# Block sums of x on GpSimd or VectorE, copies of x out of one PSUM tile in sequence, and a new compute order for the front

## The chip, the cores and the metric

The kernel runs on one core of a Trainium2 chip. The core has a matrix engine (TensorE, PE in the profile; PEld is its weight load), three engines for element-wise work (VectorE = DVE, ScalarE = ACT, GpSimd = POOL), and SyncE (SP), which here only issues DMAs. Each engine runs its own instructions strictly in program order and waits on semaphores for the others. Operands lie in SBUF (128 partitions); matmul results lie in PSUM, in eight banks. The metric is the device time of one execution in microseconds, the median of several.

## What is computed

Linear attention with the feature map elu+1 on 8 batches of 8 heads, 576 tokens, 64 features; its output, laid out as 4608 tokens of 512 features, goes through a mixture of 8 experts whose routing weights are balanced by eight Sinkhorn rounds.

```python
def _attn_ref(q, k, v):                       # (8, 8, 576, 64)
    def phi(x): return np.where(x > 0, x, np.exp(x) - 1.0) + 1.0
    q_p, k_p = (phi(q), phi(k))
    kv = np.einsum('bhsd,bhse->bhde', k_p, v)
    z = np.sum(k_p, axis=2)
    num = np.einsum('bhsd,bhde->bhse', q_p, kv)
    den = np.einsum('bhsd,bhd->bhs', q_p, z)[..., None] + 1e-06
    return (num / den)
def _moe_ref(x, w_gate, w1, w2):              # 4608 tokens, D 512, E 8, F 1024
    P = np.exp(logits - logits.max())         # logits = x @ w_gate; then 8 rounds of row and column scaling
    for e in range(E):
        h = np.maximum(x @ w1[e], 0.0)
        out += P[:, e:e + 1] * (h @ w2[e])
```

## The kernel before, in words

**Stages.** The *front* (0 to about 121 us of the span) is the attention, in 16 half batches (`att(b, g)`, n = 2b + g, each one batch and four heads). The matrix work of the first expert on the first token groups is mixed in between as filler. Then come the other experts. Tokens are worked in 9 groups g of 512. For expert 0 the groups 0 to 4 are done plainly: `layer1` (L637, hq: x times w1, then relu L641 on ACT) and the second layer (L906, ye: h times w2, then a copy to `acc`, L260 on ACT or L262 on DVE). Groups 5 to 8 of expert 0 and all later experts use a seven-product (Strassen-like) scheme for the first layer, `block7` (L783, L788), and, for later experts, for the second (L1044). From 170 us on the matrix work of all later experts runs in one fixed sequence.

**One half batch of the front.** DMAs bring k and q (one tile `kqin`, two buffers) and v (`vin`, two buffers). From n = 2 to 5 all three, and later v alone, are issued from POOL's queue; the others from SP's. ACT takes exp of k and of q (L311), DVE forms max(1 + x, 1) (L324, fp32 in, fp16 out) and then min with the exp (L327, two fp16 tiles of SBUF in). v is copied to `vv` (L260 on ACT or L262 on DVE). PE forms k'v (L356), copied to `kvz` by either engine; PE turns q over (L212), copied to `qpT` by either engine. PE forms the numerators and denominators (L414, in two parts); 1e-6 is added (`rden`, L424 on ACT or L426 on DVE), DVE takes the reciprocal (L429) and multiplies (`xn`, L438). PE turns `xn` over into one PSUM tile (L212), and two copies take it to `xT` in SBUF: `f_xc`, one instruction for s = 0 and one for s = 1, on ACT (L260) or DVE (L262). For n = 0 the two lie in two tiles, for n > 0 in one.

**Block sums.** The seven-product scheme needs sums and differences of blocks of x. `x_blocks(g)` makes four tiles T[0] to T[3] from `xT` of its 512 tokens with four subtractions of 128 x 512 fp16 (L675, L676 in the first task, i = 0; L678 in the second; L680 in the third), all on DVE. `f_st` and `f_raw` then send T and x to DRAM from SP's queue (tile `xd`); later experts read them back from there (`x_load`, L712). Groups 0 to 4 ("early") put T into a part of the accumulator tile `acc[6]`, two halves in turn; groups 5 to 8 into `xst`, two buffers, after the memory of the front is free (`t_close`), and expert 0 reads these T directly in `block7`. The column `acc` in the profile's L675 to L680 rows is this use of `acc[6]`.

**The order.** Every piece of work is a task with a number, dependencies, buffer groups, and a planned cost for each engine that may run it (`_Plan.add`). `_Plan.run(order)` takes a text with one list of task numbers for each engine: pool, pe, sp, dma (planned transfers, no instruction), act and dve. A task with several engines in its cost table runs on the one whose list holds it. Within an engine the list is the program order. The dependencies in the plan only shape the sequence in which the tasks are written out; the semaphores are placed by the tile framework from the real reads and writes, and two engines that read one PSUM tile are also put in sequence. The lists cover the front, expert 0 and the start of expert 1; the rest follows from priorities in the plan, with the matrix work of the later experts chained in one fixed sequence.

Of the kernel before, what the change touches and what calls it, by code (L numbers as in the profile page):

```python
# [139 lines left out]
def kernel(  # L140
# [136 lines left out]
    def att(b, g):  # L277
# [186 lines left out]
        for s in range(2):  # L464
            w, o = (256, 320)[s], S * b + 256 * s

            def f_xc(e, s=s, w=w, o=o):
                copy(e, xT[:, 2 * g:2 * g + 2, o:o + w],
                     gxn["ps"][s][:, 0:640].rearrange("p (c t) -> p c t", c=2)[:, :, 0:w])
            t2 = fadd({"act": (0.56, 0.65)[s], "dve": (0.38, 0.46)[s]}, f_xc, deps=[t1], use=[gxs[s % len(gxs)]], prio=pr)  # L470
            for c2 in range(2):
                xt_done.setdefault((b, 2 * g + c2), []).append(t2)

# [178 lines left out]
    def x_blocks(g):  # L652
# [9 lines left out]
                nc.sync.dma_start(out=xd[g // 2][:, g % 2, 1 + b], in_=xT[:, 2:4, t0 + 256 * b:t0 + 256 * b + 256])  # L662
        last = first = None
        for i in range(3):
            def f_T(_, i=i):
                if i == 0 and early:
                    h_ = (len(p_xse["order"]) - 1) % 2
                    gt_["tile"] = (acc[NA - 1][:, 2 * h_:2 * h_ + 2, :].bitcast(FP16)
                                   .rearrange("p a (b c t) -> p (a b) c t", b=2, c=2))
                elif i == 0:  # L670
                    gt_["tile"] = accp[2].tile([P, 4, 2, 256], FP16, tag="xst", name="xst")
                T = gt_["tile"]
                lo, hi = xT[:, :, t0:t0 + 256], xT[:, :, t0 + 256:t0 + 512]
                if i == 0:
                    nc.vector.tensor_tensor(out=T[:, 0], in0=hi[:, 0:2], in1=lo[:, 0:2], op=ALU.subtract)  # L675
                    nc.vector.tensor_tensor(out=T[:, 2], in0=hi[:, 2:4], in1=hi[:, 0:2], op=ALU.subtract)  # L676
                elif i == 1:
                    nc.vector.tensor_tensor(out=T[:, 1], in0=hi[:, 2:4], in1=T[:, 0], op=ALU.subtract)  # L678
                else:
                    nc.vector.tensor_tensor(out=T[:, 3], in0=lo[:, 2:4], in1=T[:, 1], op=ALU.subtract)  # L680
            last = add(("dve", 0.8 if i == 0 else 0.42), f_T,
                       deps=deps + [v_land[NG + 1 + g] if early else t_close, last] +
                       ([xst_of[g - 1][2]] if i == 0 and g > NG - NL else []),
                       acq=[gt_] if i == 0 else [], use=[gt_], prio=g - 8.0)
            first = first or last
            x_users.append(last)
# [455 lines left out]
    for d, k_ in zip(chain, chain[1:]):  # L1142
        S_.dep(k_, d)

    order = """
        pool 0 50 102 104 106 108 110 137 139 141 169 171 175 177 554 179 206 208 210 241 272 305 336 367 398 431 462
        493 524 534 586 583 1571 1091 1580 1573 1582 1584 1575 1119 1117 1093 1577 1240 1216 1586 1214 1242 1337 1339
        1363 1365
        pe 2 3 4 5 6 7 8 9 10 11 12 13 14 15 16 17 18 51 54 19 20 21 22 62 23 58 24 25 26 86 83 94 27 28 29 30 31 90 66
# [24 lines left out]
        act 42 43 75 76 82 87 84 68 112 113 100 143 629 631 144 637 121 150 639 633 152 635 641 643 127 654 181 136 182  # L1174
# [11 lines left out]
        dve 44 46 45 49 47 55 77 56 52 78 63 59 64 79 80 65 60 61 88 91 95 67 92 96 93 114 97 115 116 99 119 117 124 145  # L1186
# [15 lines left out]
    """  # L1202
    S_.run(order)

# [29 lines left out]
```

## Time and profile before

| | |
|---|---|
| time, median of 3 runs | 953.49 us (953.34 to 954.19) |
| the profiled execution | 953.06 us; its span from first to last instruction 951.2 us |
| busy in the span | PE 938.1 us (99%), DVE 768.6 us (81%), ACT 565.1 us (59%), POOL 161.7 us (17%) |
| granted TensorE clock | 1.000 |
| the 36 block-sum subtractions on DVE (L675 to L680) | 0.40 to 0.42 us each |
| two-input adds on POOL (L1068, 128 x 256 fp32), x124 | 852 ns mean, 726 ns median |

The profiled execution lies 0.43 us under the median of the runs; the span is 1.86 us shorter than the execution's own time. A matmul's end is modelled, 380 ns after its start for 512 columns, although the next one starts 216 ns after it; so short pauses of PE are hidden in its busy time, and the distance from one start to the next is the better reading.

### The profile page before, as it was taken

Reading aid. Unit: us, or ns where it says so; the run is one execution under the profiler, and the core shown is the slowest. Engines: PE = TensorE matmul, PEld = TensorE weight load, DVE = VectorE, ACT = ScalarE, POOL = GpSimd, SP = SyncE. Lnnn points to the kernel's source line nnn. Section 1 sums busy time; section 2 is a strip of 40 time slices with the busy share of each in tenths; the row PEclk is TensorE's granted clock in tenths of the full one; section 3 lists DMA queues with packets and bytes.
Section 4 is the critical chain, followed back from the end, with each engine's and each line's share of the span. In section 5 each row is a group of like instructions: output and inputs, shape, how many; then the busy total and the mean of one; then the engine's idle time right before and its main releaser. Section 6 shows DMA issues by size and latency. Waiting matters only on the chain.

```text
span 951.2 us, 19287 instructions
## 1 busy us (share of the span) xinstructions
PE 938.1 (99%) x7524; PEld 631.7 (66%) x7524; DVE 768.6 (81%) x1527; ACT 565.1 (59%) x1023; POOL 161.7 (17%) x209
## 2 busy tenths in 40 slices
PE   6999999999999999999999999999999999999998
PEld 3555567466676667766676667766676666766676
DVE  6899988788887787878887787887877788877776
ACT  4799755665655555555555555555555555555551
POOL 3211100022222211221112211221112211111111
PEclk9999999999999999999999999999999999999999
DMA  9998965253254422544145431644125532425545
GB/s 310 302 270 245 222 193 182 50 103 85 65 149 111 111 68 62 111 111 101 57 132 116 102 84 44 135 111 101 56 77 103 109 96 56 139 79 161 150 107 133
DMA packets 109948, 118.91 MB, mean 125 GB/s; under 512 B 7840, under 2 KB 95520, under 8 KB 109856
## 3 DMA queue, kind: packets, MB, share of 16 engines
q1 hardware_dynamic: 81600, 90.33, 31.2%
q0 software_dynamic: 27856, 26.82, 16.9%
q8 instruction: 59, 0.97, 0.4%
q10 hardware_dynamic: 400, 0.52, 0.2%
q14 instruction: 33, 0.27, 0.1%
HBM read 119.69 MB, written 17.69 MB: 144 GB/s over the span
## 4 chain that ended last, share of the span: by engine, by line
PE 94%; DMA 2%; ACT 1%; DVE 1%; issue 0%; SPq 0%; DVEq 0%; ACTq 0%
PE ye L1044 34%; PE hq L783 20%; PE att L783 10%; PE ye L906 6%; PE Zye L1044 6%; PE Zye L783 5%; PE hq L788 4%; PE hq L637 3%; PE att L788 2%; DMA kqin<-in_k_dram 1%; PE Zye L788 1%; DMA vin<-in_v_dram 1%; PE kv_ps L212 1%; PE kv_ps L356 1%; PE kv_ps L414 1%; DVE xn L438 0%
## 5 line engine op out<-in xcount | busy, mean ns | idle before, releaser
L1058 DVE SCALAR_TENSOR_TENSOR acc<-ye,P_sb,acc 128x256 f32<-128x256 f32 x620 | 267.3, 477 | 101.9 <-PE ye L1044 99.9
L1044 PEld LDWEIGHTS <-S 128*128 128x128 f16 x1984 | 194.1, 98 | 45.9 <-issue 0.3
L1068 POOL TENSOR_TENSOR acc<-acc,h 128x256 f32<-128x256 f32 x124 | 103.6, 852 | 601.2 <-ACT h L1065 595.8
L1044 PE MATMUL ye<-h,S 128*128 128x256 f16 x1488 | 192.8, 273 | 0.0
L1044 PEld LDWEIGHTS <-h 128*128 128x128 f16 x1488 | 145.6, 98 | 39.9
L823 ACT ACTIVATE h<-hq 128x512 f16<-128x512 f32 x134 | 80.1, 598 | 137.1 <-PE hq L783 116.9
L783 PEld LDWEIGHTS <-W 128*128 128x128 f16 x896 | 87.7, 98 | 81.2
L783 PE MATMUL att<-xs,W 128*128 128x512 f16 x448 | 133.2, 379 | 0.0
L783 PE MATMUL hq<-xs,W 128*128 128x512 f16 x448 | 133.2, 379 | 0.0
L783 PE MATMUL hq<-xs,w 128*128 128x512 f16 x448 | 124.1, 379 | 0.0
L826 DVE CUSTOM_DVE_ANT_0 h<-att,s 128x512 f16<-128x512 f32 x126 | 86.2, 686 | 21.8 <-ACT s L810 19.2
L783 PEld LDWEIGHTS <-w 128*128 128x128 f16 x672 | 65.8, 98 | 54.5
L820 ACT ACTIVATE h<-Zye 128x512 f16<-128x512 f32 x134 | 80.1, 597 | 34.0 <-PE Zye L783 28.1
L803 ACT COPY Zye<-hq 128x512 f32<-128x512 f32 x134 | 77.9, 581 | 33.5 <-PE hq L783 26.8
L826 DVE CUSTOM_DVE_ANT_0 h<-hq,s 128x512 f16<-128x512 f32 x126 | 86.4, 686 | 12.3 <-PE hq L783 12.2
L1065 ACT ACTIVATE h<-Zye,P_sb 128x256 f32<-128x256 f32 x124 | 52.3, 470 | 72.5 <-PE Zye L1044 72.5
L810 ACT COPY s<-hq 128x512 f32<-128x512 f32 x126 | 73.5, 584 | 35.0 <-PE hq L783 30.6
L1015 DVE TENSOR_TENSOR S<-h 128x1024 f16<-128x1024 f16 x124 | 85.1, 687 | 6.9 <-ACT h L823 6.9
L817 ACT COPY s<-att 128x512 f32<-128x512 f32 x126 | 74.6, 592 | 1.3 <-PE att L783 1.3
L906 PE MATMUL ye<-w,h 128*128 128x512 f16 x296 | 74.2, 380 | 0.0
L783 PE MATMUL Zye<-xs,w 128*128 128x512 f16 x224 | 66.6, 379 | 0.0
L1044 PE MATMUL ye<-w,h 128*128 128x256 f16 x496 | 64.3, 273 | 0.0
(123 smaller groups left out, 1048.8 us busy)
## 6 DMA issues: line engine op xcount, KB each, us to landing
xs<-xd SPq DMA_DIRECT2D x196, 256.0 KB, 4.2
w<-in_moe_w_dram POOLq DMA_DIRECT2D x48, 256.0 KB, 4.3
out_dram<-acc SPq DMA_DIRECT2D x67, 128.0 KB, 2.4
kqin<-in_k_dram SPq DMA_DIRECT2D x12, 576.0 KB, 5.6
kqin<-in_q_dram SPq DMA_DIRECT2D x12, 576.0 KB, 7.1
xs<-xd SPq DMA_DIRECT2D x49, 128.0 KB, 2.7
xd<-xT SPq DMA_DIRECT2D x27, 128.0 KB, 3.2
vin<-in_v_dram POOLq DMA_DIRECT2D x10, 288.0 KB, 6.8
```

What stands on the lines that cost most here:

```text
L783: nc.tensor.matmul(dst, lhsT=lhs(0, c), rhs=X(b)(c), start=(first and c == 0), stop=(c == 1), skip_group_check=True)
L803: nc.scalar.copy(out=Zt[1], in_=gX["tile"])
L810: nc.scalar.copy(out=gs2["tile"], in_=gX["tile"])
L817: nc.scalar.copy(out=gs5["tile"], in_=gR["tile"])
L820: nc.scalar.activation(out=hd(0, 0), in_=Zt[1], func=AF.Relu)
L823: nc.scalar.activation(out=hd(1, 0), in_=gX["tile"], func=AF.Relu)
L826: nc.vector._custom_dve(TENSOR_ADD_SAT, out=dst, in0=ps, in1=sb, s0=3.0e38, s1=0.0)
L906: nc.tensor.matmul(gy[tt]["tile"], lhsT=hx(f, P * tt, P), rhs=gw2["tile"][:, f, :], start=(f == 0), stop=(f == NFT - 1))
L1015: nc.vector.tensor_tensor(out=gS[i]["tile"], in0=a0, in1=a1, op=op)
L1044: nc.tensor.matmul(bank(g_)[:, s, :], lhsT=lhs(s, kk), rhs=rhs(kk), start=(new and s == 0 and kk == 0), stop=(kk == 3), skip_group_check=True)
L1058: nc.vector.scalar_tensor_tensor(out=dst(), in0=bank(g_)[:, s, :], scalar=P_sb[:, gg, e:e + 1], in1=dst(), op0=ALU.mult, op1=ALU.add)
L1068: nc.gpsimd.tensor_tensor(out=dst(), in0=dst(), in1=gst["tile"], op=ALU.add)
```

## The change

Three parts.

1. `x_blocks`: the four subtractions of a group may run on POOL as well as on DVE. In the new lists POOL runs 28 of the 36: all four of the groups 0, 1, 2, 4, 6 and 8, and the first two of the groups 3 and 7. The rest (the last two of groups 3 and 7, all of group 5) stay on DVE. 18 of the 28 belong to early groups.
2. `f_xc`: in the plan, the copy of s = 1 depends on the copy of s = 0 when both come from one PSUM tile.
3. The lists for pool, pe, act and dve are replaced. The lists for sp and dma are as they were. 35 tasks go from ACT to DVE and 35 from DVE to ACT (copies, `rden` additions, one `xn`, scalings of `acc`); the rest changes place only.

```diff
-            t2 = fadd({"act": (0.56, 0.65)[s], "dve": (0.38, 0.46)[s]}, f_xc, deps=[t1], use=[gxs[s % len(gxs)]], prio=pr)
+            t2 = fadd({"act": (0.56, 0.65)[s], "dve": (0.38, 0.46)[s]}, f_xc, deps=[t1, t2 if s and n else None], use=[gxs[s % len(gxs)]], prio=pr)
...
-            def f_T(_, i=i):
+            def f_T(eng, i=i):
...
+                v_ = nc.gpsimd if eng == "pool" else nc.vector
                 lo, hi = xT[:, :, t0:t0 + 256], xT[:, :, t0 + 256:t0 + 512]
                 if i == 0:
-                    nc.vector.tensor_tensor(out=T[:, 0], in0=hi[:, 0:2], in1=lo[:, 0:2], op=ALU.subtract)
-                    nc.vector.tensor_tensor(out=T[:, 2], in0=hi[:, 2:4], in1=hi[:, 0:2], op=ALU.subtract)
+                    v_.tensor_tensor(out=T[:, 0], in0=hi[:, 0:2], in1=lo[:, 0:2], op=ALU.subtract)
+                    v_.tensor_tensor(out=T[:, 2], in0=hi[:, 2:4], in1=hi[:, 0:2], op=ALU.subtract)
...
-            last = add(("dve", 0.8 if i == 0 else 0.42), f_T,
+            last = add({"dve": 0.75 if i == 0 else 0.42, "pool": 3.6 if i == 0 else 1.8}, f_T,
...
-        pool 0 50 102 104 106 108 110 137 139 141 169 171 175 177 554 179 206 208 210 241 272 305 336 367 398 431 462
-        493 524 534 586 583 1571 1091 1580 1573 1582 1584 1575 1119 1117 1093 1577 1240 1216 1586 1214 1242 1337 1339
+        pool 0 50 102 104 106 108 110 137 139 141 169 171 175 177 554 179 206 208 210 241 272 305 336 367 398 588 589
+        431 590 462 595 596 493 597 524 602 534 586 603 604 609 616 583 617 848 849 850 900 618 952 953 954 1571 1091
```

In the pool list 367 and 398 are the v loads of n = 10 and 11; 431, 462, 493 and 524 those of n = 12 to 15; 534 waits for v of n = 15; 586 and 583 load weights of expert 1, 1571 of expert 2. 588 to 590 are the three tasks of group 0, 595 to 597 of group 1, 602 to 604 of group 2, 609 the first of group 3, 616 to 618 of group 4, 848 to 850 of group 6, 900 the first of group 7, 952 to 954 of group 8.

More of the change, by code (lines that the diff above doesn't have):

```diff
@@ L672, in f_T @@
                 T = gt_["tile"]
+                v_ = nc.gpsimd if eng == "pool" else nc.vector
                 lo, hi = xT[:, :, t0:t0 + 256], xT[:, :, t0 + 256:t0 + 512]
                 if i == 0:
-                    nc.vector.tensor_tensor(out=T[:, 0], in0=hi[:, 0:2], in1=lo[:, 0:2], op=ALU.subtract)
-                    nc.vector.tensor_tensor(out=T[:, 2], in0=hi[:, 2:4], in1=hi[:, 0:2], op=ALU.subtract)
+                    v_.tensor_tensor(out=T[:, 0], in0=hi[:, 0:2], in1=lo[:, 0:2], op=ALU.subtract)
+                    v_.tensor_tensor(out=T[:, 2], in0=hi[:, 2:4], in1=hi[:, 0:2], op=ALU.subtract)
                 elif i == 1:
-                    nc.vector.tensor_tensor(out=T[:, 1], in0=hi[:, 2:4], in1=T[:, 0], op=ALU.subtract)
+                    v_.tensor_tensor(out=T[:, 1], in0=hi[:, 2:4], in1=T[:, 0], op=ALU.subtract)
                 else:
-                    nc.vector.tensor_tensor(out=T[:, 3], in0=lo[:, 2:4], in1=T[:, 1], op=ALU.subtract)
-            last = add(("dve", 0.8 if i == 0 else 0.42), f_T,
+                    v_.tensor_tensor(out=T[:, 3], in0=lo[:, 2:4], in1=T[:, 1], op=ALU.subtract)
+            last = add({"dve": 0.75 if i == 0 else 0.42, "pool": 3.6 if i == 0 else 1.8}, f_T,
                        deps=deps + [v_land[NG + 1 + g] if early else t_close, last] +
@@ L1145 @@
     order = """
-        pool 0 50 102 104 106 108 110 137 139 141 169 171 175 177 554 179 206 208 210 241 272 305 336 367 398 431 462
-        493 524 534 586 583 1571 1091 1580 1573 1582 1584 1575 1119 1117 1093 1577 1240 1216 1586 1214 1242 1337 1339
-        1363 1365
-        pe 2 3 4 5 6 7 8 9 10 11 12 13 14 15 16 17 18 51 54 19 20 21 22 62 23 58 24 25 26 86 83 94 27 28 29 30 31 90 66
[11 rows of a table removed]
+        pool 0 50 102 104 106 108 110 137 139 141 169 171 175 177 554 179 206 208 210 241 272 305 336 367 398 588 589
+        431 590 462 595 596 493 597 524 602 534 586 603 604 609 616 583 617 848 849 850 900 618 952 953 954 1571 1091
+        1580 1573 1582 1584 1575 1119 1117 1093 1577 1240 1216 1586 1214 1242 1337 1339 1363 1365
+        pe 2 3 4 5 6 7 8 9 10 11 12 13 14 15 16 17 18 54 51 62 19 58 20 86 21 22 23 24 83 25 66 94 90 26 27 624 28 29
[11 rows of a table added]
         1159 1161 1163 1100 1167 1169 1165 1171 1175 1177 1103 1173 1181 1183 1179 1110 1112 1115 1185 1120 1123 1187
@@ L1173 @@
         1587 1387 1389 1391 1502 1504 1506 1508
-        act 42 43 75 76 82 87 84 68 112 113 100 143 629 631 144 637 121 150 639 633 152 635 641 643 127 654 181 136 182
[11 rows of a table removed]
-        dve 44 46 45 49 47 55 77 56 52 78 63 59 64 79 80 65 60 61 88 91 95 67 92 96 93 114 97 115 116 99 119 117 124 145
[15 rows of a table removed]
+        act 42 43 75 52 76 88 91 95 67 97 112 113 100 629 631 143 637 144 121 150 639 152 635 633 641 127 643 654 181
[11 rows of a table added]
+        dve 44 46 47 49 45 77 56 55 79 78 59 63 80 60 64 61 65 82 87 84 92 68 96 93 114 99 116 119 117 145 115 146 147
[14 rows of a table added]
     """
```

73 rows, old and new, of the table order are left out of this document.

## The prediction

> **What bounds the kernel now.** I read the busy time by stage first, since the page's averages mix them.
>
> ```profile
> core 0: us, PE busy (x) PEld busy (x) DVE busy (x) ACT busy (x) POOL busy (x), PEclk, DMA share, GB/s
> 0.00:27.00 27.00, 19.56 (x235) 9.51 (x236) 17.61 (x39) 13.60 (x15) 11.95 (x21) 1.00 1.00 311
> 27.00:67.00 40.00, 39.79 (x573) 20.49 (x572) 36.86 (x73) 35.01 (x56) 5.88 (x8) 1.00 1.02 289
> 67.00:121.00 54.00, 53.10 (x857) 28.54 (x856) 49.54 (x109) 45.96 (x72) 5.67 (x8) 1.00 0.96 233
> 121.00:170.00 49.00, 48.63 (x349) 33.44 (x347) 43.12 (x104) 27.00 (x51) 0.74 (x1) 1.00 0.55 173
> 170.00:951.00 781.00, 777.05 (x5518) 539.77 (x5516) 621.42 (x1206) 443.50 (x832) 137.47 (x171) 1.00 0.41 100
> ```
>
> From 170 us on PE has no room (in the chain of waits its matmuls follow each other at 109 ns per 256 columns). Before 27 us the inputs are on their way (DMA share 1.00). The front from 27 to 121 us is where the change can act: DVE is busy 86.4 of 94 us there, ACT 81.0, POOL 11.6. PE looks full, but its ends are modelled, so I count its work from matmul groups.
>
> ```profile
> L637 PE MATMUL hq<-xT,w 128*128 128x512 f16 x80 | 20.2, 380 | 0.0
> L906 PE MATMUL ye<-w,h 128*128 128x512 f16 x77 | 19.4, 381 | 0.0
> ```
>
> These are the groups of 67 to 121. Four such matmuls follow each other in 0.87 us, so 157 need 34.1 us. The small ones, by the least distance from one task's start to the next in the timeline: 8 k'v at 0.53, 16 turnings at 0.27, 8 pairs of numerators at 0.32, 3 logits at 0.90, together 13.8. That is 47.9 of 54 us, so PE has about 6 us of pauses here; the same count for 27 to 67 gives 36.3 of 40. Both lists of PE hold the same work up to the last logits of the front, and behind it PE is full: a microsecond by which the front gets shorter or longer is a microsecond of the kernel, and the pauses cap the gain at 10 us. DVE's largest groups in 67 to 121 (two-input min and max of the front), then its longest waits in 27 to 121 (us in total, times, longest):
>
> ```profile
> L327 DVE TENSOR_TENSOR t<-t,e 128x1152 f16<-128x1152 f16 x14 | 10.4, 750 | 0.2
> L324 DVE TENSOR_SCALAR t<-kqin 128x1152 f16<-128x1152 f32 x12 | 9.2, 769 | 0.1
> ```
>
> ```profile
> DVE xT L262 <- ACT xT L260: 2.5, 6, 0.6
> DVE rden L426 <- PE kv_ps L414: 2.1, 4, 1.1
> ```
>
> DVE waits only 5.9 us in all; it is the fullest engine, and 2.5 us of its waiting is for ACT's copy out of the same PSUM tile.
>
> **Part by part. Off DVE.** Block sums stand on DVE like this:
>
> ```profile
> 87.96 0.42 DVE L675 TENSOR_TENSOR acc<-xT 128x512 f16<-128x512 f16 x1
> 88.30 0.42 DVE L676 TENSOR_TENSOR acc<-xT 128x512 f16<-128x512 f16 x1
> 88.64 0.41 DVE L675 TENSOR_TENSOR acc<-xT 128x512 f16<-128x512 f16 x1
> ```
>
> Each lasts 0.42 us but the next starts 0.34 after it; I take 0.08 off every DVE duration for this. DVE's list up to its last x copy held 17 subtractions and holds none now: -17 x 0.336 = -5.7 us.
>
> **Between ACT and DVE.** Counted in the two lists up to the same point, with the rows' means: DVE gets 4 `qpT` copies (0.753), 3 `vv` copies (1.65 together), 2 copies to `acc` (0.678); it loses 2 `kvz` (0.421), 4 `rden` (0.164) and one `xn` (0.688): +3.8, less 0.1 for overlap. DVE's net is -2.0 us. ACT gets about 5.7 us lighter; the one `xn` on ACT is 8 small multiplications, not in the trace, between 8 x 0.24 and 8 x 0.28 by the smallest ACT rows. ACT was not the fuller engine, so I count nothing for it.
>
> **x copies in sequence.** In the old lists 13 of 16 half batches have their two x copies on two engines, in the new ones 7. That gives back between 0 and 2.9 us of DVE's waits for ACT (2.5, and 0.4 for exp); I take 1.5, because the waits at L414 may grow instead.
>
> **POOL's own time.** No row shows 128 x 512 fp16 on POOL. The nearest is L1068, 128 x 256 fp32: 0.72 us undisturbed, so between 0.72 and 1.44; I take 1.3, since a copy of 4 columns takes 0.21, which leaves 0.51 per 256. Can POOL keep up? In its queue the sums stand between v loads:
>
> ```profile
> 67.81 0.71 POOL L295 DMA_DIRECT2D vin<-in_v_dram  x1 [2.26 <-DVE rden L429]
> 76.28 0.70 POOL L295 DMA_DIRECT2D vin<-in_v_dram  x1 [7.76 <-DMA vin<-in_v_dram]
> 80.08 1.06 POOL L295 DMA_DIRECT2D vin<-in_v_dram  x1 [3.10 <-ACT kvz L260]
> ```
>
> Three sums (3.9 us) go into the gap of 7.8, one (1.3) into the next of 3.1, three into 6.4, one into 8.5: no v load is late, even at 1.7 each. On SP the store of group 0 (before at 78.8 us) waits for the sum behind v of n = 12, so at 76.98 + 1.3 = 78.3; the k and q loads queued behind it came at 81.1. The store of group 1 comes earlier than its 94.0. The weight loads 586 and 583, at 104 us before, slip by up to 12 us; the first `W` made of them stands at 142.6 on DVE. Group 6 on POOL follows the end of the front by 4 x 1.3 = 5.2 us, to 126; PE reads it at about 134. So the move hides, as long as nothing else holds POOL.
>
> **POOL and DVE at once.** This decides. Two places where POOL's add meets a two-input DVE instruction (the `S` sums, of the same kind as L327):
>
> ```profile
> 242.24 0.69 DVE L1015 TENSOR_TENSOR S<-h 128x1024 f16<-128x1024 f16 x1
> 242.96 1.10 DVE L1015 TENSOR_TENSOR S<-S,h 128x1024 f16<-128x1024 f16 x1
> 244.09 0.69 DVE L1015 TENSOR_TENSOR S<-h,S 128x1024 f16<-128x1024 f16 x1
> ```
>
> ```profile
> 242.31 1.19 POOL L1068 TENSOR_TENSOR acc<-acc,h 128x256 f32<-128x256 f32 x1 [5.34 <-DVE h L985]
> ...
> 257.98 0.73 POOL L1068 TENSOR_TENSOR acc<-acc,h 128x256 f32<-128x256 f32 x1 [5.99 <-ACT h L1065]
> ```
>
> POOL's add began inside the first `S` and took 1.19 instead of 0.72; the next `S` then took 1.10 instead of 0.69. At 257.98 POOL began first, an `S` at 258.39 (by the same timeline) took 0.87, 0.18 too long: it was held until 0.59 us into POOL's instruction. So each holds the other up. For 512 columns the hold lies between 0.59 and 2 x 0.59 = 1.18; I take 1.0. In DVE's new list behind n = 10, instructions of SBUF operands alone (L324, L327, `vv`) are 17.3 of 42.6 us, some 25 starts. Spread evenly (0.6 starts a microsecond) they lose on average 0.25 us to one hold of 1.0 us; averaged over every place of the list, with the runs they form there and POOL starting when one of them ends, 0.41. Both ends count: 0 if every hold meets PSUM work, 1.0 if every hold is lost. I take 0.36, nearer the list: 18 early subtractions x 0.36 = 6.5 us, of which 15% falls into DVE's pauses (4.5 of 54 us, and some at the end): +5.5. That L324 and the copies are held like L327 is not in the trace for a sum; two L324 beside a DMA issue of POOL took 0.89 and 0.97 instead of 0.75.
>
> The Trainium skill states the rule that speaks against the change (SBUF — State Buffer, section Who interferes with whom): GpSimd shares a pair of SBUF ports with VectorE, and an instruction in a two-port mode, or with two SBUF inputs beside a GpSimd read, is blocked for the whole of the other one. The `S` rows agree with it in kind; the 0.59 of 0.72 us is a little less than the whole. With the whole 1.3 us as the hold, the same average is about 0.55, the term 18 x 0.55 x 0.85 = 8.4 in place of 5.5, and the time 958.7.
>
> **Behind the front** 10 more subtractions leave DVE (-3.4) and cost about 10 x 0.36 there; DVE is 88% busy and PE hardly waits for it (chain: one wait of 0.4 us): +0.3, bounds -0.3 and +1.5. The first 67 us are reordered with the same work: 0, bounds -2 and +2 (the PE pauses there are 3.7).
>
> **Sum.** -2.0 - 1.5 + 5.5 + 0.3 = +2.3 us on the profiled 953.06: 955.4, and with the 0.43 to the median of the runs 955.8 us.
>
> **Rivals.** *The relief wins* (other side): the sums fall beside PSUM work (L438, `qpT`, x copies), or only L327 is held (under half of the 25 starts) and most of that in pauses. Then 953.5 - 2.0, less 1.5 to 2.9 for the waits, plus 0 to 1.5 for holds: 948.6 to 951.5, say 950.0. For it: 59% of DVE's list time is no such instruction, ACT is lighter by 5.7, fewer copies wait across engines. Against: L324 and L327 come in runs. *They cancel*: 953.5. *A late T stops PE*: the first sum of group 7 (900) waits in POOL's queue until PE has left the tile of group 5 at about 132 us, and the last sum of group 4, group 8 and a weight load stand behind it. If POOL needs over 2 us for each, group 8 is late by some 4 us at its first use, PE stops there, and it is 955.8 + 4 = 960. Against: group 7 was done at 138 before, group 8 at 154. *The sums don't run on POOL*: excluded by the lists, which name the engine.
>
> **Numbers.** Differences under 0.2% (1.9 us) count as none. The forecast (slower, its own range 954.5 to 959) has 0.48, of which 0.08 lies inside 0.2%; relief 0.36, of which 0.02 inside; cancel 0.10; late T 0.06. So faster 0.34, same 0.20, slower 0.46. The low end of the range has no hold, all 2.9 us of waits back and the early stage at -2: 953.5 - 2.0 - 2.9 - 0.3 - 2.0 = 946.3. The high end has 0.6 us a hold, no waits back and +1.5 behind the front: 953.5 - 2.0 + 9.2 + 1.5 = 962.2. I give 946.5 to 962; a hold of 1.0 each is left to the rest.
>
> **What would show it.** Right: L324 and L327 rows over 0.9 us beside POOL subtractions, sums on POOL mostly 1.3 to 1.8 us, the last logits of the front (L485, 120.05 us before) 1 to 5 us later, the stage after 170 unchanged. Wrong: L327 stays at 0.75, or the last logits come before 118 us, or PE waits at L788 for a POOL tile.

## The result, and the profile after

The changed kernel takes 967.42 us (median of 4 runs, 966.36 to 968.73) against 953.83 us (953.34 to 954.19) for the kernel before: a ratio of 1.0144, 95% interval 1.0126 to 1.0161. It is slower, as forecast, but by 13.6 us instead of 2.3, and outside the range given. The profiled execution took 966.98 us, with a span of 965.1 us (before 951.2). From L661 on its line numbers are higher by one: the block sums are now L676 to L681.

Busy time by stage, as shown of before (engines, granted clock PEclk, DMA share, GB/s), with five short stretches inside:

```profile
core 0: us, PE busy (x) PEld busy (x) DVE busy (x) ACT busy (x) POOL busy (x), PEclk, DMA share, GB/s
67.00:121.00 54.00, 45.87 (x655) 23.57 (x653) 47.37 (x79) 35.88 (x58) 20.59 (x21) 0.91 0.79 199
72.00:74.00 2.00, 1.32 (x22) 0.54 (x22) 2.00 (x1) 1.98 (x4) 2.00 (x3) 1.00 1.07 326
74.00:76.00 2.00, 0.00 (x0) 0.00 (x0) 2.00 (x3) 0.28 (x1) 0.22 (x1) 0.86 0.60 101
76.00:78.00 2.00, 1.16 (x18) 0.75 (x19) 2.00 (x8) 0.00 (x0) 0.00 (x0) 0.50 0.00 0
78.00:80.00 2.00, 2.00 (x7) 0.68 (x5) 1.77 (x3) 0.68 (x2) 0.00 (x0) 0.50 0.61 132
80.00:82.00 2.00, 2.00 (x28) 0.90 (x27) 0.19 (x2) 2.00 (x3) 0.00 (x0) 0.50 1.04 412
...
170.00:951.00 781.00, 780.76 (x5554) 543.12 (x5553) 625.75 (x1215) 454.33 (x851) 136.56 (x170) 1.00 0.40 99
```

In 67 to 121 PE lost 7.2 us of busy time (53.10 before). Between 74 and 76 it ran nothing, and then, from 76 to 82, it had half its clock. From 80 to 82 DVE is idle: now PE is late for it. The stage behind 170 is as before.

The costliest groups, for 67 to 132.5, where the front now ends:

```profile
L637 PE MATMUL hq<-xT,w 128*128 128x512 f16 x76 | 21.5, 420 | 0.6 <-ACT h L641 0.6
L907 PE MATMUL ye<-w,h 128*128 128x512 f16 x83 | 21.2, 384 | 0.0
L327 DVE TENSOR_TENSOR t<-t,e 128x1152 f16<-128x1152 f16 x15 | 15.3, 1032 | 0.2
L324 DVE TENSOR_SCALAR t<-kqin 128x1152 f16<-128x1152 f32 x13 | 13.7, 1056 | 0.2 <-DMA kqin<-in_k_dram 0.2
```

The means of L327 and L324 went from 750 and 769 ns to 1032 and 1056. It is not that all of them are slower: two instructions are. DVE's timeline (start, duration) shows them, and POOL's shows what ran meanwhile:

```profile
69.74 0.75 DVE L327 TENSOR_TENSOR t<-t,e 128x1152 f16<-128x1152 f16 x1
70.40 4.45 DVE L324 TENSOR_SCALAR t<-kqin 128x1152 f16<-128x1152 f32 x1
...
84.02 4.91 DVE L327 TENSOR_TENSOR t<-t,e 128x1152 f16<-128x1152 f16 x1
```

```profile
70.12 0.71 POOL L295 DMA_DIRECT2D vin<-in_v_dram  x1 [5.58 <-DVE vv L262]
70.85 1.17 POOL L676 TENSOR_TENSOR acc<-xT 128x512 f16<-128x512 f16 x1
71.96 1.16 POOL L677 TENSOR_TENSOR acc<-xT 128x512 f16<-128x512 f16 x1
73.08 1.15 POOL L679 TENSOR_TENSOR acc<-xT,acc 128x512 f16<-128x512 f16 x1
...
83.07 1.17 POOL L681 TENSOR_TENSOR acc<-xT,acc 128x512 f16<-128x512 f16 x1
84.17 0.74 POOL L295 DMA_DIRECT2D vin<-in_v_dram  x1
...
87.15 1.15 POOL L679 TENSOR_TENSOR acc<-xT,acc 128x512 f16<-128x512 f16 x1
```

L324 began while POOL issued a v load, and it came through only after the third sum. The second long instruction, the L327 at 84.02, lies in the same way over a sum that itself follows a v load (at 82.31), a second v load and three more sums (up to 88.30); it began inside the first of these sums. I call such a stay a hold. Together the two lost 3.70 + 4.16 = 7.9 us. PE's longest waits, of which before had none over 0.3 us, follow from them:

```profile
PE kv_ps L356 <- DVE t L327: 3.6, 1, 3.6
PE kv_ps L414 <- DVE qpT L262: 3.5, 1, 3.5
```

Up to half batch 7 the new kernel was 1.6 us ahead (last x copy 69.7, before 71.3 us). By half batch 8 it was 11.0 us late (94.7, before 83.7): nearly all is lost in the stretch with the two long instructions. The last logits of the front (L485) begin at 131.85 us, 11.8 later than the 120.05 of before; behind them 2.1 us more are lost up to the end of the span (13.9).

### The profile page after: what moved, and what is told of

Same layout as the page of the kernel before. It is cut to its first block, busy times and chain, and to the rows that moved or that the text cites. A ratio compares the mean times of both kernels' runs of the same rounds, so it can differ in the third digit from the quotient of the medians.

```text
span 965.1 us, 19302 instructions
## 1 busy us (share of the span) xinstructions
PE 944.7 (98%) x7524; PEld 633.6 (66%) x7524; DVE 776.8 (80%) x1499; ACT 562.0 (58%) x1030; POOL 193.8 (20%) x237
## 4 chain that ended last, share of the span: by engine, by line
PE 90%; DVE 5%; DMA 2%; ACT 2%; issue 1%; SPq 0%; ACTq 0%; DVEq 0%
PE ye L1045 33%; PE hq L784 20%; PE att L784 10%; PE Zye L1045 6%; PE Zye L784 5%; PE ye L907 5%; PE hq L789 3%; PE hq L637 2%; PE att L789 2%; DMA kqin<-in_k_dram 1%; DVE t L327 1%; ACT e L311 1%; DVE t L324 1%; PE Zye L789 1%; PE kv_ps L212 1%
## 5 line engine op out<-in xcount | busy, mean ns | idle before, releaser
L824 ACT ACTIVATE h<-hq 128x512 f16<-128x512 f32 x134 | 80.1, 598 | 135.9 <-PE hq L784 117.1
L821 ACT ACTIVATE h<-Zye 128x512 f16<-128x512 f32 x134 | 80.1, 597 | 35.3 <-PE Zye L784 26.4
L827 DVE CUSTOM_DVE_ANT_0 h<-hq,s 128x512 f16<-128x512 f32 x126 | 86.4, 685 | 12.0 <-PE hq L784 11.8
```

The costliest lines, as they stand in the source:

```text
L821: nc.scalar.activation(out=hd(0, 0), in_=Zt[1], func=AF.Relu)
L824: nc.scalar.activation(out=hd(1, 0), in_=gX["tile"], func=AF.Relu)
L827: nc.vector._custom_dve(TENSOR_ADD_SAT, out=dst, in0=ps, in1=sb, s0=3.0e38, s1=0.0)
```

## The experiments

Times are medians, each beside runs of the kernel before on the same chip. "Front" is the start of the last matmul of the last logits (L485) in the profiled execution (before: 120.9 us; the changed kernel: 132.7).

**The lists alone, and the move alone.** In e1 the new lists stay, and the sums run on DVE:

```diff
-                v_ = nc.gpsimd if eng == "pool" else nc.vector
+                v_ = nc.vector
```

> The changed kernel with its lists as they are, but the block sums run on VectorE in their places of the POOL list's order (the task waits are the same, only the engine that executes the subtraction differs). Theory of the holds (DVE is passed over while POOL runs block sums, and PE's clock falls in the pauses that follow): the two stays of 4.4 and 4.9 us at L324 and L327 vanish, the granted clock stays at 1.00 from 67 us on, and the time is 951 to 955 us, since the front had been 1.6 us ahead at half batch n=7 and some 20 x 0.34 us of subtractions go back onto DVE. Rival, the new compute orders themselves cost the 13.6 us: 963 us or more with the same delay at n = 8 to 10.

957.24 us (ratio 1.0034, 1.0020 to 1.0049), front at 124.8. No L324 or L327 is long, and the clock is 1.00 from 67 us on. It is some 2 us above the forecast of the holds theory: without the holds the front still ends 3.9 us later than before. Not all of that is the lists. In this profiled run the granted clock was 0.53 from 10 to 15 us and 0.50 from 15 to 20 (before: 1.00; changed kernel: 0.90 and 0.76), and half batch 7 ends 1.3 us later than in the changed kernel with the same lists (last x copy 71.0 against 69.7). That leaves some 2.6 us for the lists, with the sums at the places where POOL's list put them.

In e2 the lists of before stay, but for the 20 sum tasks that go into POOL's:

```diff
-                    nc.vector.tensor_tensor(out=T[:, 0], in0=hi[:, 0:2], in1=lo[:, 0:2], op=ALU.subtract)
+                    v_.tensor_tensor(out=T[:, 0], in0=hi[:, 0:2], in1=lo[:, 0:2], op=ALU.subtract)
...
-        pool ... 367 398 431 462 493 524 534 586 583 1571 ...
+        pool ... 367 398 588 589 431 590 462 595 596 493 597 524 602 534 586 603 604 609 616 583 617 848 ...
```

> The kernel before with its own orders of PE, ACT, DVE and SP; only the 20 block-sum tasks are moved from DVE's list into POOL's, at the places which they have there in the changed kernel, and no order between the two x copies is added. Theory of the holds: some instructions of L324 or L327 stay for 2 us or more beside runs of POOL sums, and the time is 957 to 970 us. Rival, the new orders are what costs: 951 to 955 us, as DVE has 5.7 us less to do and its list is the old one.

967.16 us (1.0141, 1.0124 to 1.0158), front at 134.0: the move alone costs as much as the whole change. Up to half batch 6 the tasks stand some 0.6 us behind their old times; then come the holds, in DVE's timeline:

```profile
69.11 3.97 DVE L327 TENSOR_TENSOR t<-t,e 128x1152 f16<-128x1152 f16 x1
...
85.62 4.34 DVE L324 TENSOR_SCALAR t<-kqin 128x1152 f16<-128x1152 f32 x1
...
107.77 3.13 DVE L324 TENSOR_SCALAR t<-kqin 128x1152 f16<-128x1152 f32 x1
```

Each one lies over two or three sums that follow a v load; a further one of 2.41 us (at 80.56) lies over a single sum.

**The added wait between x copies.**

```diff
-... f_xc, deps=[t1, t2 if s and n else None], ...
+... f_xc, deps=[t1], ...
```

> The changed kernel without the one added wait between the x copies of the two half batches in a group (one engine at a time). Both theories: 966 to 969 us, as the orders already put the copies so; if the wait itself were what costs, 955 us or less.

967.92 us in one run, inside the changed kernel's 966.36 to 968.73, with the same two holds (4.44 and 5.69 us): no cost of the wait is seen.

**What makes a hold long.** While the holds of before 90 us lasted through several sums, at 131 to 137 us the same two engines took turns. I suspected the DMA issue in front. m1 measures this by itself; nothing of the reference is computed in it. Each phase starts both engines together; these are the sequences of POOL (D a DMA issue, S a sum, w a 4-column copy that waits for ScalarE) and of DVE (p a copy from PSUM, m a min like L327, c a fp16 copy); some of the 18 phases:

```python
("dSl", "DSSS", "ppmmmmmm"),
...
("sS6", "SSSSSS", "pmmmmmmmm"), ("dS6", "DSSSSSS", "pmmmmmmmm"), ... ("dSw", "DSwSwS", "pmmmmmm"),
... ("cd", "DSSS", "pcccccc"), ... ("pd", "DSSS", "ppppppp"), ...
```

> A measurement by itself: nothing of the reference is computed, the output is zeros. Phases with a common start, in each of which VectorE runs one PSUM copy and then 4 to 10 equal instructions, POOL nothing, 3 or 6 sums of 128x512, or the same directly behind a DMA issue, or with a copy of 4 columns or a wait for ScalarE between them. Theory of the chain behind a DMA issue: with sums alone each VectorE instruction of two SBUF operands waits at most 1.1 us; with the issue right ahead the first one waits for all sums (3 sums: 4 us, 6 sums: 7.5 us); a wait for another engine behind the issue or between the sums brings the turns back. Rival, back-to-back sums alone shut VectorE out: 3 sums cost 3 us with or without the issue. Rival, turns always: no instruction above 2.0 us anywhere.

DVE's timeline in m1 (L69 is the min, L73 the copy, L67 the copy from PSUM), in this order: the first min of dSl, which becomes ready only inside the first sum behind D; two mins beside six sums alone; the first min behind D and six sums; two mins where POOL waits between its sums; the first fp16 copy behind D and three sums; seven PSUM copies beside the same:

```profile
36.17 3.50 DVE L69 TENSOR_TENSOR tdSl<-e,vv 128x1152 f16<-128x1152 f16 x1
...
58.35 1.26 DVE L69 TENSOR_TENSOR tsS<-e,vv 128x1152 f16<-128x1152 f16 x1
...
59.65 1.59 DVE L69 TENSOR_TENSOR tsS<-e,vv 128x1152 f16<-128x1152 f16 x1
...
71.68 7.64 DVE L69 TENSOR_TENSOR tdS<-e,vv 128x1152 f16<-128x1152 f16 x1
...
108.89 2.13 DVE L69 TENSOR_TENSOR tdSw<-e,vv 128x1152 f16<-128x1152 f16 x1
...
111.06 1.73 DVE L69 TENSOR_TENSOR tdSw<-e,vv 128x1152 f16<-128x1152 f16 x1
...
146.98 4.03 DVE L73 COPY tcd<-e 128x1152 f16<-128x1152 f16 x1
...
165.75 5.04 DVE L67 CAST bpd<-ps 128x512 f16<-128x512 f32 x7
```

An undisturbed min takes 0.76. Beside sums alone the engines take turns: each min takes 1.59, so one sum costs DVE 0.83 us, and the sum itself stretches from 1.15 to 1.66. With the DMA issue right in front the first min stays for the whole run, 7.64 us for six sums, and POOL loses nothing (1.14 to 1.16 a sum). The min need not be ready during the issue: in dSl it becomes ready 0.49 us into the first sum, as in the phase of sums alone (58.35, with the sum begun at 57.85), and is held through all three sums, where without the issue it took 1.26. In another phase one that becomes ready inside the second of three sums is held to the end of the third as well (2.28). Copies of 4 columns between the sums don't break the run (4.58 us for three), a pause of 0.29 us in which POOL waits does. The fp16 copy and L324's kind (4.33) are held as well; PSUM copies are not (0.69 each). A DMA issue with no sum behind it held nothing (0.75). A second pass through all phases gave these rows again within 0.02 us, but for dSl's 3.50, which was 3.61. The theory holds, also in size; of its two waits that should bring the turns back, only the one between the sums was tried, as POOL did not pause at the one behind the issue.

**Without the DMA issue in front, in the kernel.** e4 is e2 with a POOL copy that reads the just loaded v ahead of five groups of sums:

```diff
+                if (g, i) in behind:
+                    nc.gpsimd.tensor_copy(out=gate, in_=vin_t[behind[(g, i)]][:, 0, 0, 0:4])
```

> As e2 (the kernel before's own orders, the block sums on POOL), but in front of each of the five groups of sums that follow a v load in POOL's queue stands a copy of 4 columns on POOL that reads the loaded v, so that POOL pauses some 2 to 4 us between issuing the load and the first sum. Theory of the chain behind a DMA issue (a VectorE instruction that is pending while POOL issues a DMA, or runs the sum right behind it, is passed over until POOL pauses; without a DMA issue right ahead the two engines take turns): no L324 or L327 above 2.0 us, the two or three long stays of 2.4 to 4.3 us become delays of 0.5 to 1.1 us each, and the time is 954 to 959 us. Rival, any run of POOL sums back to back shuts VectorE out: still stays of 3 us and more, 963 to 968 us.

965.47 us (1.0121, 1.0102 to 1.0139): the time says rival, the trace says theory. No L324 or L327 is above 1.72 us, and up to half batch 9 nothing is lost but 0.8 us from before the first sum. But my gate was badly chosen, as POOL's timeline shows:

```profile
68.59 0.71 POOL L296 DMA_DIRECT2D vin<-in_v_dram  x1 [2.25 <-DVE rden L430]
75.91 0.18 POOL L677 CAST gate<-vin 128x4 f32<-128x4 f16 x1 [6.62 <-DMA vin<-in_v_dram]
...
79.91 0.74 POOL L296 DMA_DIRECT2D vin<-in_v_dram  x1
```

A v load takes 7 us to land here, so the sums came late and the next v loads behind them too: issued at 79.9, 85.4 and 96.9 instead of 76.3, 80.1 and 87.5. The dearest wait came by SP's queue. There the store of T waits for the group's last sum, and the next k load stands right behind the store. For group 1 this is SP, then ACT's exp that waits for this k load, then PE:

```profile
103.45 0.34 SPq L695 DMA_DIRECT2D xd<-acc  x1
103.95 0.37 SPq L296 DMA_DIRECT2D kqin<-in_k_dram  x1
...
110.84 1.16 ACT L312 ACTIVATE e<-kqin 128x1152 f16<-128x1152 f32 x1 [5.33 <-DMA kqin<-in_k_dram]
...
112.54 1.01 PE L638 MATMUL hq<-xT,w 128*128 128x512 f16 x2 [3.61 <-ACT h L642]
```

Before, the two stood at 94.05 and 94.50. Between half batches 11 and 12 the delay grows from 3.6 to 9.1 us. A new wait took the old one's place. One long hold is left, at the end of the front: a block sum of DVE takes 4.11 us (at 129.69) beside four sums of POOL behind a weight load.

e5 opens the groups with a copy that reads a result of DVE or ACT instead, and puts groups into POOL's idle gaps:

```diff
+                    nc.gpsimd.tensor_copy(out=gate, in_=t_of[n]["tile"][:, 0, 0, 0:4] if wh == "t" else
+                                          z_of[n]["tile"][:, 0, 0, 0:4] if wh == "z" else xT[:, 0, 6 * S:6 * S + 4])
-        ... 398 588 589 431 590 462 595 596 493 597 524 602 534 586 603 604 609 616 583 617 848 ...
+        ... 398 588 589 590 431 462 595 596 493 597 602 524 603 604 534 586 583 609 616 617 848 ...
```

> As e2 (the kernel before's own orders of PE, ACT, DVE and SP, the block sums on POOL), but POOL's sums stand in its idle gaps between v loads: each of five groups begins with a copy of 4 columns that reads a result of DVE or ACT which is ready 0.5 to 2 us behind the last DMA issue, so that POOL has been idle and no v load has to wait long. The weight loads 586 and 583 stand ahead of groups 3 and 4. Theory of the chain behind a DMA issue, with turns otherwise: each sum that meets SBUF work holds DVE for 0.83 us and gives it back 0.34 us of subtraction; with 40 to 65% of the 17 early sums met, 17 x (0.33 to 0.54 - 0.34) = 0 to +3.5 us, so 953 to 958 us, no L324 or L327 above 2.0 us up to 110 us, and the granted clock at 1.00 from 67 us on. Rival, the sums on POOL cost some 10 us wherever they stand: 960 us or more. Rival, relief: 951 us or less.

959.26 us (1.0053, 1.0036 to 1.0069), 5.0 above the kernel before, where e2 was 13.9 above, and 1.3 above the forecast's upper end; front at 126.6. The clock did not stay at 1.00: it was 0.50 from 76 to 78 us. DVE and POOL take turns now, as in these rows of DVE (two lines were added above, so L326 is L324):

```profile
71.96 1.76 DVE L326 TENSOR_SCALAR t<-kqin 128x1152 f16<-128x1152 f32 x1
...
75.26 1.70 DVE L326 TENSOR_SCALAR t<-kqin 128x1152 f16<-128x1152 f32 x1
```

All rows of DVE from 67 us to the last x copy together lie 7.2 us above the medians that the same kinds of row had before, and in the changed kernel 7.9, which is all in the two long instructions; both are 5.7 lighter in subtractions. So e5's front is 5.7 us late for a net loss of 1.5, and the changed kernel's, without some 2.6 for its lists (e1), 11.8 - 2.6 = 9.2 us late for a net loss of 2.2. That asks what a loss in lumps of 4 us costs besides its length.

**What a lump costs.** e6 gives PE work in the two pauses: matmuls whose results are overwritten.

```diff
+                if (g, f, e) == (2, 6, 0):
+                    for _ in range(17):
+                        nc.tensor.matmul(ghq["tile"], lhsT=xT[:, 0, 0:P], rhs=xT[:, 0, 0:512], start=True, stop=True)
...
+            if n == 11:
+                for _ in range(15):
+                    nc.tensor.matmul(gkv["tile"][:, 0], lhsT=xT[:, 0, 0:P], rhs=xT[:, 0, 0:512], start=True, stop=True)
```

> The changed kernel with extra matmuls whose results are overwritten: 17 of 128x512 ahead of the layer-1 task at 72.3 us and 15 ahead of the k'v task at 89.0 us, so that PE is busy in the two pauses of 3.5 and 3.6 us in which VectorE is held. They add 7 us of PE work in pauses and change nothing else. Theory: the two holds cost twice, once as lost VectorE time and once because PE runs at a granted clock of 0.50 for some 5 and 3 us behind each pause; with PE kept busy the clock stays at 1.00, and the time falls by 3 to 5 us, to 962.5 to 964.5 us. Rival: VectorE alone sets the pace behind the holds, and the clock costs nothing: 966 to 968.5 us.

963.91 us (1.0128, 1.0097 to 1.0160); one of four runs took 969.38. So it was run again beside the changed kernel:

> The changed kernel once more, beside e11 on one chip, as the base that e11 is compared with: 966 to 968.5 us, the granted clock at 0.50 behind both holds.

> The kernel of e6 (32 extra matmuls in the two pauses of PE) once more with more rounds, since one of its four runs lay 5 us above the others. Theory that the half clock behind the holds costs time: 2.5 to 5 us below e10. Rival, VectorE alone sets the pace there: within 1 us of e10.

e10: 968.32 us (1.0158, 1.0138 to 1.0178). e11: 964.73 us (1.0126, 1.0105 to 1.0146), 3.6 lower; the intervals overlap a little (1.0138 to 1.0146), with one run of 969.57. Of the nine runs of e6 and e11 seven took 963.1 to 964.8; all nine of the changed kernel (four of the result, five of e10) took 966.4 to 971.6. The windows of e6 behind the first hold have the full clock where the changed kernel had 0.50:

```profile
72.00:77.00 5.00, 5.00 (x39) 2.28 (x38) 5.00 (x10) 1.62 (x2) 1.40 (x2) 1.00 0.53 115
77.00:82.00 5.00, 5.00 (x61) 2.44 (x59) 5.00 (x11) 4.42 (x6) 1.41 (x2) 1.00 0.70 239
```

The holds are still there (4.44 and 6.05 us, the second 1.1 longer), so the gain is not theirs: 32 matmuls that compute nothing save 3.6 us. e11's profile happens to be the run of 969.57, and DVE's timeline tells why: two later runs of sums caught DVE as well.

```profile
104.42 3.35 DVE L324 TENSOR_SCALAR t<-kqin 128x1152 f16<-128x1152 f32 x1 [0.60 <-DMA kqin<-in_k_dram]
...
112.17 2.40 DVE L327 TENSOR_TENSOR t<-t,e 128x1152 f16<-128x1152 f16 x1
```

e7 and e8 make lumps without POOL: in the kernel before, instructions of L324 and L327 are executed 12 more times: one of each line six more times, in two lumps (e7, below), or all twelve of half batches 10 to 12 once more each, over 69 to 88 us (e8).

```diff
+                for _ in range(1 + RT.get((n, a0), 0)):
+                    nc.vector.tensor_scalar(out=tv(gtt), in0=kv_in(gkq), scalar1=1.0, scalar2=1.0, op0=ALU.add, op1=ALU.max)
...
+                for _ in range(1 + RM.get((n, a0), 0)):
+                    nc.vector.tensor_tensor(out=tv(gtt), in0=tv(gtt), in1=kv_in(ge), op=ALU.min)
...
+RT = {(10, 0): 6}
+RM = {(11, 1): 6}
```

> The kernel before, block sums on VectorE, with 12 VectorE instructions executed again (same inputs, same result): one L324 at 69.4 us 6 more times and one L327 at 82.6 us 6 more times, 2 x 6 x 0.67 = 8.0 us in two lumps like the two holds. Theory that lumps cost more than their length (PE pauses, and its clock falls behind them): 11 to 14 us more, 964.5 to 967.5 us, with a granted clock under 0.9 between 72 and 92 us. Rival, VectorE's time is worth its length wherever it is lost: 8 us or a little less more, 959.5 to 961.5 us.

> As e7, but the same 12 repetitions are spread: each L324 and each L327 of half batches 10 to 12 (69 to 88 us) runs twice, 8.0 us in all. Theory that lumps cost more than their length: 5 to 8 us more here, 958.5 to 961.5 us, with the granted clock at 1.00. Rival, VectorE's time is worth its length wherever it is lost: the same time as e7 within 1.5 us.

e7: 965.26 us (1.0124, 1.0109 to 1.0139). e8: 962.87 us (1.0095, 1.0080 to 1.0110). Lumps of 8.0 us cost 11.6, as expected; spread, the same 8.0 cost 9.2, more than I expected, and 2.4 less than in lumps, more than the rival allows. The mean granted clock differs between e8's runs: the profiled one, at 0.999, took 960.90, 7.2 above the kernel before, the other three, at 0.992 to 0.996, 962.55 to 963.39. The windows of e7, then those of e8:

```profile
72.00:77.00 5.00, 1.10 (x36) 1.10 (x36) 4.86 (x8) 1.38 (x3) 0.00 (x0) 0.74 0.46 103
77.00:82.00 5.00, 4.70 (x43) 2.35 (x44) 3.79 (x12) 2.29 (x5) 0.00 (x0) 0.58 0.71 236
```

```profile
72.00:77.00 5.00, 3.85 (x46) 1.82 (x45) 4.93 (x13) 3.14 (x5) 0.87 (x1) 1.00 0.87 275
77.00:82.00 5.00, 3.71 (x53) 2.00 (x54) 4.97 (x11) 3.23 (x6) 0.71 (x1) 1.00 0.48 67
```

So DVE time in this stage costs about its length wherever it is lost, and two lumps that empty PE cost some 2 to 4 us more together. The intervals of e7 and e8 just touch; e6 and e11 carry the point with them.

**A version better than both?** e9 leaves groups 0 and 1 on DVE and puts only the later sums on POOL, gated as in e5 (the lists of e5, then those of e9):

```diff
-        pool ... 398 588 589 590 431 462 595 596 493 597 602 524 603 604 534 586 583 609 ...
+        pool ... 398 431 462 493 524 602 603 604 534 586 583 609 ...
```

> The kernel before's own orders; the sums of groups 0 and 1 stay on DVE where they were, and those from group 2 on (9 of the 17 early subtractions, and the later ones) are on POOL, in its idle gap behind the last v load and behind the weight loads, each of the two early runs opened by a copy of 4 columns that reads a result of DVE or ACT, so that no run stands right behind a DMA issue. Theory of turns (a sum that meets SBUF work holds DVE 0.83 us): 9 x 0.34 = 3.0 us come off DVE and 3 to 5 us of holds go on: 953 to 956 us. Rival, relief where the holds fall into pauses and beside PSUM work: 949.5 to 952 us, a version better than both kernels.

957.03 us (1.0033, 1.0021 to 1.0045): a miss, 1.0 above the range for turns, and no relief. Nine subtractions leave DVE (3.0 us), but its rows up to the last x copy lie 3.2 us above their medians. Some 2 us of delay in the profiled run are older than its first sum on POOL; but in the one run of e9 with a mean clock of 1.000 the time was 955.64, still above the 952.5 to 953.6 of such runs before. The fastest kernel of the study is the one before.

## Why the prediction was wrong in size

Its direction and the place were right: the sums on POOL and VectorE's SBUF instructions stand in each other's way, and this outweighs the relief.

- **DVE's list, -5.7 and +3.7, and x copies in sequence, -1.5.** e1 has the subtractions back on DVE and so tests +3.7 - 1.5 = +2.2 together: the front ends 3.9 us later, or some 2.6 without the low clock at its start. The sum fits; no run parts the two terms or tests -5.7 alone. Of the copies little came: in e1 DVE's waits for ACT's x copy are gone, but all its waits in 27 to 125 sum to 6.5 us (1.2 of them of a block sum for a DMA), from 5.9 before. In the changed kernel its waits at L426, L429 and for `qpT` in 27 to 132.5 sum to 9.1 us, up from 2.6 (L429 was not in the list). I had named that possibility and chosen against it; the holds add to it.
- **POOL's own time, 1.3 us: a little high.** Undisturbed sums take 1.15 to 1.17. That they would stretch to 1.3 to 1.8 holds for turns only.
- **The holds, 18 x 0.36 x 0.85 = +5.5: the step that failed.** It took a hold to end with its sum, at 1.0 us, averaged over starts to 0.36, and left even "a hold of 1.0 each" outside the range. Measured, DVE lost 7.9 us up to the last x copy, not far from the 6.5 before the share for pauses; but that is luck. All of it fell on two instructions (3.70 and 4.16 us), as a v load stood right ahead of the sums and DVE got no turn between them. I had read the POOL queue with its v loads only to ask whether a load would be late.
- **No term for PE's clock.** I let stalls cost their length. These two emptied PE for 3.5 us each, and its clock fell to 0.50 behind them: 3.6 us by e11 against e10.

With these, the front adds up only in part: 2.6 (lists) - 5.7 (sums off DVE) + 7.9 (holds) + 3.6 (clock) = 8.4 of the 11.8 us by which its last logits are late. This is an account from separate runs, and the remaining 3.4 are not assigned. Later k loads are a candidate that no run tried: the chain that ended last runs over one that SP issued at 98.7 us (before 86.2) and that landed 7.2 us later. Behind the front I had +0.3 with +1.5 at most, and it was 2.1. There the engines take turns (DVE's sums at 132.5 and 133.8 us take 1.37 instead of 0.42); no run tested that stretch alone. The rule of the Trainium skill that I weighed (SBUF — State Buffer, section Who interferes with whom: blocked for the whole instruction) fits the turns, at 0.83 to 1.03 us for a sum of 1.15. The 958.7 us that it gave is close to e5's 959.26, where only turns are left, and far from the changed kernel; but it counts the new lists, which e5 does not have, so the closeness proves little.

Of the rivals, relief is refuted by the changed kernel and, for two other placings of the sums, by e5 and e9, and the late T did not come about: no wait of PE at L789 (L788 before) ends with POOL.

## What to carry to other kernels

Moving work from VectorE to GpSimd saved its duration on VectorE only where GpSimd's run met PSUM work; beside SBUF work each 128x512 sum took back 0.83 us for the 0.34 it saved. Before placing such a run, look at what stands right ahead of it in GpSimd's queue: behind a DMA issue it shut VectorE out until GpSimd paused, in lumps of 4 us. Look, too, at what waits for the moved work in other queues: in e4 a store that waited for a late sum held the next k load behind it. And price a stall by what it empties: in 67 to 136 us of these profiles every pause of PE of 2.6 us or more was followed by half its clock, and two of 3.5 us were paid a second time with 3.6 us.

## What the runs showed of the hardware that was not expected

- A min of 0.76 us that becomes ready while GpSimd issues a DMA takes 7.64 us if six sums follow, 4.35 if three do, and 0.75 if none does. It is held also when it becomes ready inside the run. A GpSimd wait of 0.29 us is enough to let it in; in e11 a gap of 0.09 us between two sums was (113.94 to 114.03; the L327 that had begun at 112.17 ended at 114.57).
- PE's clock fell after shorter pauses than the two of 3.5 us. The Trainium skill (TensorE: Matmul & The Clock Gate, section What's actually happening) puts it at an idle window of about 3.4 us. In e2 a pause of 2.6 us (71.56 to 74.14) was followed by 0.50 from 74 to 80 us, one of 2.1 us in the same run (110.80 to 112.86) by no drop, and in e5 thin PE work with no pause above 1.3 us by 0.50 from 76 to 78. So a pause shorter than the page's window can be enough here.
- The kernel before itself varied from 952.45 to 955.54 us over these runs, and the mean granted clock goes with it: 1.000 in runs of 952.5 to 953.6, 0.994 to 0.996 in runs of 954.0 to 955.5. In the experiments' profiles the low stretch lies between 10 and 25 us, where PE waits for inputs (0.50 and 0.53 from 15 to 25 us in e9, which was some 2 us late before its first sum ran).
